# Chunk 4's attention value product of batches 1 to 6 as a Strassen product over key chunk pairs, query halves and channel halves

## The chip, the cores and the metric

The kernel runs on one core of one Trainium2 chip. The metric is the device time of one execution in microseconds (us); lower is better. Three runs of the kernel before took 1174.89 to 1175.7 us, median 1175.52.

## The reference

```python
def _attn_ref(u, v, z):
    B, S, D = u.shape            # 8, 3008, 256; z is 8 x 3008 x 64
    scale = 1.0 / S
    scores = scale * np.matmul(z, z.transpose(0, 2, 1))
    attn = np.maximum(scores, 0.0) ** 2
    out = np.matmul(attn, v)
    return (u * out).astype(np.float32)

def _moe_ref(x, w_in, w_out):    # 24064 x 256, 256 x 2048, 2048 x 256
    h = x @ w_in
    g = h * (1.0 / (1.0 + np.exp(-1.702 * h)))
    return (g @ w_out).astype(np.float32)
```

The second function is applied to the first one's output, with all batches' rows one below the other. The attention weights are symmetric, since queries and keys are the same z, and there is no softmax.

## The kernel before

**Tiles.** A batch has 3008 positions: 24 key blocks of 128 (NJ = 24; the last holds 64), and 6 query chunks of 512 (NCH = 6; the last holds 448). CB = 4 key blocks make one chunk. The 256 channels are two halves of 128 (NCC = 2), read from V with a step of two elements. All matmul operands are fp16, and sums are fp32 in PSUM.

**Scores.** `scores` (L244) computes a pair of key blocks against a query chunk on TensorE, `square` (L265, L279) takes relu with a factor csc on ScalarE and squares on VectorE. Since the weights are symmetric, only the blocks on one side of the diagonal are computed: `turn_unit` transposes a squared pair with a DMA into the tile TT, which serves as the other side's weights. `pieces` says in which order the pairs of a chunk come, the tables SCHED and SCHED0 at which step of which chunk each is issued.

**Attention value product.** `attend` (L376) computes, for a query chunk, out transposed: channels on the partitions, 512 queries along the row, summed over the key blocks in a PSUM bank for each channel half. In chunks 0 to 3 and 5 the two channel halves run side by side on two row halves of the array (64 rows each). In chunk 4 (`full(b)`, batches 0 to 6) each step is one matmul with all 128 rows: 23 key blocks for one half, then for the other, and a step for the half block, 47 steps in all. `gate` (L393) multiplies the bank by u, transposed by `turn_u` (L211), into XT, the expert's input. The bank stays taken until then.

**Up-projection inside chunk 4.** In batches 0 to 6, chunk 4's steps are interleaved with 16 groups of `up_group` (LAGY = 16): four matmuls of 512 columns (L431), a gelu on ScalarE from PSUM (L444) into one of two buffers gf, and a rescaling by FSC to fp16 on VectorE (L450), which frees gf. `some_sums` inserts sums for the down-projection behind some of them. The other 32 groups of a batch follow after chunk 5, interleaved with the down-projection (`pair_product`, L604), which is itself a seven-product (Strassen) form in which the sums S1 to S4 (`pair_sum`, L561 to L570) are made on VectorE. Its sums of the weights are made once (`weight_sums`, L498).

**Order.** Each engine executes its instructions in the order in which this program writes them; the schedule is by hand. Tables hold the places: TURN (when u is transposed), LOAD (when u is loaded, on the POOL queue), SCHED (score pairs). Buffers rotate: four PSUM banks `ps1` for products, two double banks `ps2` for scores and up-projection, three buffers for rl (the relu's result), 26 for tag "a" (weights and sums), 14 for tag "tt" (transposed weights and gelu results). A new tile waits until the last reader of the tile that had its place is done.

Of the kernel before, what the change touches and what calls it, by code (L numbers as in the profile page):

```python
# [9 lines left out]
F32 = mybir.dt.float32  # L10
F16 = mybir.dt.float16
P = 128
# [3 lines left out]
def kernel(  # L16
# [36 lines left out]
    csc = 16.0  # L53
# [17 lines left out]

    ident = const.tile([P, P], F16, name="ident")
    make_identity(nc, ident)
    nil = pw.tile([P, CH], F16, name="nil", tag="gf")
    dve.memset(nil, 0.0)  # L75

# [251 lines left out]

    def full(b):

        return NCH - 2 if b < B - 1 else NCH - 1

    def attend(b, i, both=False):
# [36 lines left out]
        def step(k):  # L370
            done = []
            for m in order[k]:
                c, h, j = m
                if (k, m) == first[c]:
                    acc[c] = ps1.tile([P, CH], F32, name="o", tag="ps1")
                ins = pe.matmul(  # L376
                    acc[c][:, :n], V16[b][h, j].rearrange("p (c k) -> p k c", k=NCC)[:, c], weights(b, i, j)[h],
                    start=(k, m) == first[c], stop=(k, m) == final[c],
                )
                if k in turns:  # L380
                    behind(acc["sig"], ins)
                done.append(ins)
            if k + 1 in turns:
                acc["sig"] = post(done)
            for c in cs:
                if k == final[c][0]:
                    gate(c)
# [28 lines left out]
    def up_group(b, q):  # L416
# [34 lines left out]
        if not pair or q < LAGY and q % 4 < 3:  # L451
            some_sums(8)
# [271 lines left out]
    def pieces(b, i):  # L724

        lst = [(i, jp) for jp in range(2 * i, NU)]
        if i == NCH - 1:
            return [(i, jp) for jp in range(2 * i) if not turned(b, jp // 2)] + lst
        if b == 0:
            return lst[-2:] + lst[:-2] if turned(b, i) else lst  # L730
        k = max(len(lst) - 6, 2)
        return lst[:k] + lst[-2:] + lst[k:-2]
# [6 lines left out]
        3: {n: 1 for n in (6, 14, 32, 38)} | {NJ: 2},  # L739
# [8 lines left out]
    TURN = {(1, NJ + 4): 2, (2, NJ + 4): 3, (4, NJ + 4): 4, (5, 8): 5}  # L748
# [53 lines left out]
    for b in range(B):  # L802
# [5 lines left out]
        for i in range(NCH):  # L808
# [4 lines left out]
            for n, step in enumerate(attend(b, i, b == 0 and i == 0)):  # L813
# [28 lines left out]
                take(host, sched[i].get(n, 0))  # L842
                if i == full(b) and n >= HEAD and (n - HEAD) * LAGY // (2 * NJ - 10) >= head and head < LAGY:
                    up_group(b, head)
                    head += 1
                step()
# [64 lines left out]
```

## Time and profile before

| | |
|---|---|
| median of three runs | 1175.52 us (1174.89 to 1175.7) |
| the profiled execution | 1175.17 us |
| its span, first to last instruction | 1173.4 us |
| mean granted TensorE clock | 1.000 |
| VectorE, ScalarE, POOL busy in the span | 872.4, 837.2, 211.2 us |
| TensorE matmuls | 7996 |
| chunk 4 of batch 2 on TensorE | 350.77 to 374.85, 24.08 us |

Times inside the profile are counted from the first instruction. Engines: PE is TensorE, PEld its weight loads, DVE VectorE, ACT ScalarE, POOL GpSimd, SP SyncE. L376 is line 376 of the kernel before. A matmul's length in the profile goes to its modelled end, so neighbours overlap, and its price is the distance between two starts. A row of a group reads: line, engine, operation, output<-inputs with shapes, count | busy us, mean ns of one | idle time before them and what ended it.

### The profile page before, as it was taken

The page shows a single profiled execution, that of the slowest core. Times are in us where ns is not written, and L with a number is a line of the kernel's source. Part 1 is how long each engine was busy: PE and PEld are TensorE (multiplying, and loading weights), DVE is VectorE, ACT ScalarE, POOL GpSimd, SP SyncE. Part 2 cuts the span into 40 slices and gives each one's busy share as a digit, 9 for nine tenths or more (in the row PEclk, how much of TensorE's full clock was granted, in tenths as well). Part 3 has the DMA queues.
Part 4 walks back from the last instruction along what each step waited for, and adds up shares of the span by engine and source line. Part 5 has one row for each costly group of instructions (what it writes and reads, how often), then busy time and mean ns, then how long its engine had stood idle before and what let it go on. Part 6 is the DMA issues. An engine that isn't in the chain of part 4 may idle for free.

```text
span 1173.4 us, 20856 instructions
## 1 busy us (share of the span) xinstructions
PE 1167.2 (99%) x7996; PEld 552.9 (47%) x7996; DVE 872.4 (74%) x1386; ACT 837.2 (71%) x941; POOL 211.2 (18%) x294
## 2 busy tenths in 40 slices
PE   9999999999999999999999999999999999999998
PEld 3544454444444445444444445444444444544446
DVE  7779865888667886588865887658876588664776
ACT  7888864688647886478864787657876578672785
POOL 3033201232012310132101421024200241001000
PEclk9999999999999999999999999999999999999999
DMA  9996499854997559965499865995559965697023
GB/s 224 201 158 104 81 174 160 97 90 92 169 158 96 90 100 175 159 97 88 97 171 148 109 87 108 173 155 92 90 99 180 140 109 83 116 175 135 1 37 73
DMA packets 459027, 143.47 MB, mean 122 GB/s; under 512 B 424624, under 2 KB 453040, under 8 KB 458928
## 3 DMA queue, kind: packets, MB, share of 16 engines
q1 hardware_dynamic: 402464, 102.36, 53.4%
q0 software_dynamic: 55104, 38.49, 22.3%
q8 instruction: 62, 1.02, 0.4%
q10 hardware_dynamic: 1360, 1.31, 0.4%
q14 instruction: 37, 0.30, 0.1%
HBM read 60.29 MB, written 24.64 MB: 72 GB/s over the span
## 4 chain that ended last, share of the span: by engine, by line
PE 99%; ACT 0%; DVE 0%; issue 0%
PE o L376 41%; PE hg L431 28%; PE st L604 23%; PE sc L244 6%; PE st L652 1%; PE yp L578 1%; PE w L99 0%; ACT rl L265 0%; PE zp L135 0%; ACT ZT L143 0%; DVE zst L128 0%; DVE a L279 0%; DVE y L670 0%; ACT zst L126 0%; DVE nil L75 0%
## 5 line engine op out<-in xcount | busy, mean ns | idle before, releaser
L444 ACT ACTIVATE gf<-hg 128x1024 f32<-128x1024 f32 (+1 forms) x384 | 382.9, 1001 | 115.0 <-PE hg L431 106.6
L265 ACT ACTIVATE rl<-sc 128x1024 f16<-128x1024 f32 (+1 forms) x301 | 287.3, 993 | 173.0 <-PE sc L244 128.7
L431 PE MATMUL hg<-xt,W 128*128 128x512 f16 (+1 forms) x1408 | 353.5, 374 | 0.0
L376 PEld LDWEIGHTS <-V 64*128 64x128 f16 (+1 forms) x4098 | 219.7, 94 | 251.1 <-issue 9.1
L376 PE MATMUL o<-a,V 64*128 64x512 f16 (+3 forms) x2278 | 296.1, 368 | 0.0
L450 DVE TENSOR_SCALAR gt<-gf 128x1024 f16<-128x1024 f32 (+1 forms) x288 | 203.7, 709 | 94.5 <-ACT gf L444 92.8
L279 DVE TENSOR_TENSOR a<-rl 128x1024 f16<-128x1024 f16 (+1 forms) x266 | 178.6, 674 | 121.7 <-ACT rl L265 120.8
L204 POOL DMA_DIRECT2D uq<-in_u_dram x168 | 115.3, 695 | 728.9 <-PE sc L244 532.5
L431 PEld LDWEIGHTS <-W 128*128 128x128 f16 x1536 | 149.5, 98 | 176.6 <-issue 3.1
L376 PE MATMUL o<-tt,V 64*128 64x512 f16 (+1 forms) x1518 | 232.5, 377 | 0.0
L244 PE MATMUL sc<-ZT 64*128 64x512 f16 (+3 forms) x688 | 115.4, 356 | 0.7 <-ACT ZT L143 0.3
L604 PEld LDWEIGHTS <-WT 128*128 128x128 f16 x736 | 72.0, 98 | 79.5 <-issue 0.6
L448 ACT ACTIVATE gt<-gf 128x1024 f16<-128x1024 f32 (+1 forms) x96 | 98.1, 1022 | 3.1
L604 PE MATMUL st<-gt,W 128*128 128x512 f16 (+1 forms) x368 | 89.9, 370 | 0.0
L604 PE MATMUL st<-s,WT 128*128 128x512 f16 (+1 forms) x368 | 89.1, 370 | 0.0
L604 PE MATMUL st<-gt,WT 128*128 128x512 f16 (+1 forms) x368 | 88.8, 370 | 0.0
L604 PEld LDWEIGHTS <-W 128*128 128x128 f16 x552 | 53.8, 98 | 58.2
L393 DVE TENSOR_TENSOR xt<-o,ut 128x512 f16<-128x512 f32 x80 | 51.5, 685 | 28.9 <-PE o L376 28.8
L566 DVE TENSOR_TENSOR s<-gt 128x1024 f16<-128x1024 f16 (+1 forms) x92 | 61.9, 673 | 1.1
L570 DVE TENSOR_TENSOR s<-gt,s 128x1024 f16<-128x1024 f16 (+1 forms) x92 | 61.0, 663 | 1.9 <-DVE s L568 0.5
L568 DVE TENSOR_TENSOR s<-s,gt 128x1024 f16<-128x1024 f16 (+1 forms) x92 | 60.9, 662 | 1.5
L621 DVE SCALAR_TENSOR_TENSOR y<-st,y 128x512 f32<-128x512 f32 (+1 forms) x69 | 45.5, 662 | 19.3 <-PE st L604 18.6
(66 smaller groups left out, 672.8 us busy)
## 6 DMA issues: line engine op xcount, KB each, us to landing
out_dram<-yo SPq DMA_DIRECT2D x156, 128.0 KB, 2.8
uq<-in_u_dram POOLq DMA_DIRECT2D x140, 128.0 KB, 3.6
V<-in_v_dram POOLq DMA_DIRECT2D x35, 256.0 KB, 6.4
tt<-a SPq DMA_TRANSPOSE x232, 3.4
uq<-in_u_dram POOLq DMA_DIRECT2D x28, 112.0 KB, 4.4
out_dram<-yo SPq DMA_DIRECT2D x28, 96.0 KB, 6.5
uq<-in_u_dram SPq DMA_DIRECT2D x20, 128.0 KB, 4.4
wst<-in_moe_w_in_dram POOLq DMA_DIRECT2D x4, 512.0 KB, 5.6
```

The costliest lines, as they stand in the source:

```text
L204: eng.dma_start(uq[k * QW:(k + 1) * QW, :n // QW].rearrange("t q c k -> t q (c k)"), src[:, :, cs])
L244: pe.matmul(sc[:, r, :q1 - q0], zt[h, 2 * kp + r, :], zt[h].rearrange("d n p -> d (n p)")[:, q0:q1], start=True, stop=True,)
L265: act.activation(rl[:, :, :n], sc[:, :, :n], AF.Relu, scale=csc)
L279: dve.tensor_tensor(a[:, :, :n], rl[:, :, :n], rl[:, :, :n], ALU.mult)
L376: ins = pe.matmul(acc[c][:, :n], V16[b][h, j].rearrange("p (c k) -> p k c", k=NCC)[:, c], weights(b, i, j)[h], start=(k, m) == first[c], s ...
L431: pe.matmul(hg[:, e, :n], W1[:, c, ff * P:(ff + 1) * P], XT[b, i][:, c, :n], start=(c == 0), stop=(c == NCC - 1),)
L444: act.activation(gf[:, :, :n], hg[:, :, :n], AF.Gelu_apprx_sigmoid, scale=1.0 / FSC)
L448: act.activation(g, gf[:, :, :n], AF.Copy, scale=FSC)
L450: dve.tensor_scalar(g, gf[:, :, :n], FSC, None, ALU.mult)
L566: dve.tensor_tensor(s_, a21, a22, ALU.add)
L570: dve.tensor_tensor(s_, a12, ST[b, s, "S2", m], ALU.subtract)
L604: pe.matmul(bank, right[:, ff], lhs[:, f], start=new and ff == 0, stop=ff == NFF // 2 - 1, skip_group_check=True,)
```

## The change

In batches 1 to 6 (`split`), chunk 4's product is made by seven products of half size instead of eight. The left matrix is split in query halves (m) and key chunks of a pair (e), V in key chunks and channel halves; there are three pairs of key chunks (t), of four blocks each (g). Per batch VectorE makes for each t four forms of V (`value_forms`, into VT) and four forms of the scores (`score_forms`, S1, S2 and S4 into SA; S3 in place), at the places that `fills` lists as (chunk, step). Every product then runs over 3 x 4 blocks with 256 queries: 42 steps of two matmuls. P1, P5 and P2 begin a bank; P6, P7 and P4 are added to P1's, P3 to P5's. ScalarE copies the bank where an intermediate sum is needed (after P1, P5 and P6) into ya, which takes two of rl's three buffers; VectorE adds P7, P3 and P2 to it and multiplies by u; P4's result is multiplied from the bank. The last, half block of V is copied by POOL into VZ, a tile whose other half holds zeros, so that it counts as a whole block.

Moved with it (in batches 1 to 6 where nothing else is said): the transpose of u for chunk 4 from step 28 to step 10, in batches 1 to 7; the score pairs of chunk 3's steps 6, 14, 32 to steps 3, 10, 17; the order of the pairs of chunk 4; the down-projection's sums begin at the ninth group instead of the first, and a group now stands behind its step instead of ahead of it. The factor csc is 8 instead of 16. Batches 0 and 7 keep the old product.

```diff
--- before.py
+++ after.py
@@ -50,7 +50,7 @@
     LAST = S - (NCH - 1) * CH
     LFULL = LAST - SREM
 
-    csc = 16.0
+    csc = 8.0
     FSC = csc * csc * float(S) * float(S)
 
     dve, act, pe, sp, pool = nc.vector, nc.scalar, nc.tensor, nc.sync, nc.gpsimd
@@ -69,10 +69,12 @@
     ET = mybir.EngineType
     ctx.enter_context(tc.manual_schedule(engines={ET.PE, ET.Pool, ET.SP, ET.DVE, ET.Activation}))
 
+    VZ = const.tile([P, D], F16, name="VZ")
     ident = const.tile([P, P], F16, name="ident")
     make_identity(nc, ident)
     nil = pw.tile([P, CH], F16, name="nil", tag="gf")
     dve.memset(nil, 0.0)
+    pool.memset(VZ, 0.0)
 
     ZP, WS = {}, {}
     late, LATE = [], []
@@ -326,6 +328,156 @@
         return TT[b, cj, i][:, :, g, :]
 
 
+    def channels(v_, c):
+
+        return v_.rearrange("p (c k) -> p k c", k=NCC)[:, c]
+
+    def split(b, i):
+
+        return i == NCH - 2 and 0 < b < B - 1
+
+    VT, SA = {}, {}
+
+    def key_half(b, t, e):
+
+        last = t == NCH // 2 - 1 and e
+        js = [(8 * t + 4 * e, CB - int(last), 0)] + ([(NJ - 1, 1, CB - 1)] if last else [])
+        for j, n, g in js:
+            src = VZ.rearrange("p (o d) -> p o d", o=1) if j == NJ - 1 else V16[b][:, j:j + n]
+            yield src.rearrange("p j (c k) -> p j k c", k=NCC), g, n
+
+    def value_forms(b, t):
+
+        def form(f):
+            if t not in VT:
+                VT[t] = pa.tile([P, 4, CB, P], F16, name="vt", tag="tt", bufs=14)
+            (k1, _, _), = key_half(b, t, 0)
+            for k2, g, n in key_half(b, t, 1) if f else [(None, 0, CB)]:
+                out_, t1, t2 = (VT[t][:, x, g:g + n] for x in (f, 0, 1))
+                b11, b12 = k1[:, g:g + n, 0], k1[:, g:g + n, 1]
+                a_, b_ = (
+                    (b12, b11) if f == 0 else (k2[:, :, 1], t1) if f == 1
+                    else (k2[:, :, 1], b12) if f == 2 else (k2[:, :, 0], t2)
+                )
+                dve.tensor_tensor(out_, a_, b_, ALU.subtract)
+
+        return [lambda f=f: form(f) for f in (0, 2, 1, 3)]
+
+    def score_part(b, t, e, part, m):
+
+        i, c0 = NCH - 2, 2 * t + e
+        if c0 == i:
+            if part == 0:
+                return unit[b, i, 2 * i][:, 2 * m:2 * m + 2]
+            return unit[b, i, 2 * i + 1][:, m].rearrange("p r (q c) -> p r q c", c=P)
+        tile_ = TT[b, min(c0, i), max(c0, i)][:, 2 * m:2 * m + 2]
+        if t < NCH // 2 - 1:
+            return tile_.rearrange("p q g c -> p (q g c)")
+        tile_ = tile_[:, :, 2 * part:2 * part + 2]
+        return tile_ if part == 0 else tile_.rearrange("p q r c -> p r q c")
+
+    def score_form(b, t, name, part):
+        a11, a12, a21, a22 = (score_part(b, t, e, part, m) for m, e in ((0, 0), (0, 1), (1, 0), (1, 1)))
+        if name == "S3":
+            dve.tensor_tensor(a21, a11, a21, ALU.subtract)
+            return
+        if (t, name) not in SA:
+            SA[t, name] = pa.tile([P, 2, CH], F16, name="sa", tag="a", bufs=26)
+        if t < NCH // 2 - 1:
+            view = lambda x: SA[t, x].rearrange("p r c -> p (r c)")
+        else:
+            view = lambda x: SA[t, x][:, part].rearrange("p (q r c) -> p q r c", r=2, c=P)
+        if name == "S1":
+            dve.tensor_tensor(view(name), a21, a22, ALU.add)
+        elif name == "S2":
+            dve.tensor_tensor(view(name), view("S1"), a11, ALU.subtract)
+        else:
+            dve.tensor_tensor(view(name), a12, view("S2"), ALU.subtract)
+
+    def score_forms(b, t):
+        parts = 1 if t < NCH // 2 - 1 else 2
+        return [lambda x=x, p_=p_: score_form(b, t, x, p_) for x in ("S1", "S2", "S4", "S3") for p_ in range(parts)]
+
+    def moving(b, t, g, name):
+
+        raw = {"P1": (0, 0), "P2": (0, 1), "P4": (1, 1), "P7": (1, 0)}
+        if name in raw:
+            m, e = raw[name]
+            i, c0 = NCH - 2, 2 * t + e
+            if c0 != i:
+                return TT[b, min(c0, i), max(c0, i)][:, 2 * m:2 * m + 2, g]
+            if g < 2:
+                return unit[b, i, 2 * i][:, 2 * m:2 * m + 2, g]
+            return unit[b, i, 2 * i + 1][:, m, g % 2]
+        form = SA[t, {"P5": "S1", "P6": "S2", "P3": "S4"}[name]]
+        if t < NCH // 2 - 1:
+            return form.rearrange("p r c -> p (r c)").rearrange("p (q g c) -> p q g c", g=CB, c=P)[:, :, g]
+        part = form[:, g // 2].rearrange("p (q r c) -> p q r c", r=2, c=P)
+        return part[:, :, g % 2] if g < 2 else part[:, g % 2]
+
+    def still(b, t, g, name):
+
+        if name in ("P1", "P2", "P3"):
+            j = 8 * t + g + (0 if name == "P1" else CB)
+            return channels(VZ if j == NJ - 1 else V16[b][:, j], int(name == "P3"))
+        return VT[t][:, {"P5": 0, "P6": 1, "P7": 2, "P4": 3}[name], g]
+
+    def attend_split(b, i):
+
+        seq = [("P1", 0), ("P1", 1), ("P1", 2), ("P5", 0), ("P5", 1), ("P2", 0), ("P2", 1), ("P6", 0), ("P6", 1)]
+        seq += [("P5", 2), ("P6", 2), ("P3", 0), ("P3", 1), ("P7", 0), ("P7", 1), ("P7", 2)]
+        seq += [("P3", 2), ("P2", 2), ("P4", 0), ("P4", 1), ("P4", 2)]
+        XT[b, i] = pa.tile([P, NCC, CH], F16, name="xt", tag="xt", bufs=6)
+        banks, half = {}, CH // 2
+
+        def step(name, t, h):
+            new = name in ("P1", "P2", "P5")
+            if new and (t, h) == (0, 0):
+                banks[name] = ps1.tile([P, CH], F32, name="oz", tag="ps1")
+            bank = banks[{"P6": "P1", "P7": "P1", "P4": "P1", "P3": "P5"}.get(name, name)][:, :half]
+            for g in (2 * h, 2 * h + 1):
+                pe.matmul(
+                    bank, still(b, t, g, name), moving(b, t, g, name),
+                    start=new and (t, g) == (0, 0), stop=(t, g) == (2, CB - 1), skip_group_check=True,
+                )
+            if (t, h) != (2, 1):
+                return
+            if name == "P1":
+                banks["y"] = [pw.tile([P, 2, half], F32, name="ya", tag="rl", bufs=3) for _ in range(2)]
+            y, x = banks["y"], XT[b, i]
+            ut = lambda c: UT[b, i][:, c].rearrange("p q t -> p (q t)")
+            if new and name != "P2" or name == "P6":
+                k, r = {"P1": (1, 0), "P5": (0, 1), "P6": (0, 0)}[name]
+                act.activation(y[k][:, r], bank, AF.Copy, scale=1.0)
+            elif name == "P4":
+                dve.tensor_tensor(x[:, 0, half:], bank, ut(0)[:, half:], ALU.mult)
+            else:
+                k, r = {"P3": (0, 0), "P7": (0, 1), "P2": (1, 0)}[name]
+                part = y[k][:, r]
+                dve.tensor_tensor(part, part, bank, ALU.add)
+                if name == "P3":
+                    dve.tensor_tensor(x[:, 1], y[0].rearrange("p o c -> p (o c)"), ut(1), ALU.mult)
+                elif name == "P2":
+                    dve.tensor_tensor(x[:, 0, :half], part, ut(0)[:, :half], ALU.mult)
+
+        return [lambda x=x, t=t, h=h: step(x, t, h) for x, t in seq for h in range(2)]
+
+    def fills(b):
+
+        VT.clear()
+        SA.clear()
+        at = {(0, 19): [lambda: pool.tensor_copy(VZ[TOP], V16[b][TOP, NJ - 1])]}
+        slots = [(0, n) for n in (20, 23, 26, 28)] + [(1, n) for n in (27, 31, 35, 39, 43)]
+        slots += [(2, n) for n in (19, 21, 23)]
+        ops = [op for t in range(3) for op in value_forms(b, t)]
+        slots += [(2, n) for n in (28, 33, 38, 43)] + [(3, n) for n in (30, 34, 41, 44)]
+        slots += [(4, n) for n in (12, 12, 14, 14, 16, 18, 20, 22)]
+        ops += [op for t in range(3) for op in score_forms(b, t)]
+        assert len(ops) == len(slots)
+        for where, op in zip(slots, ops):
+            at.setdefault(where, []).append(op)
+        return at
+
     def full(b):
 
         return NCH - 2 if b < B - 1 else NCH - 1
@@ -374,7 +526,7 @@
                 if (k, m) == first[c]:
                     acc[c] = ps1.tile([P, CH], F32, name="o", tag="ps1")
                 ins = pe.matmul(
-                    acc[c][:, :n], V16[b][h, j].rearrange("p (c k) -> p k c", k=NCC)[:, c], weights(b, i, j)[h],
+                    acc[c][:, :n], channels(V16[b][h, j], c), weights(b, i, j)[h],
                     start=(k, m) == first[c], stop=(k, m) == final[c],
                 )
                 if k in turns:
@@ -448,7 +600,7 @@
             act.activation(g, gf[:, :, :n], AF.Copy, scale=FSC)
         else:
             dve.tensor_scalar(g, gf[:, :, :n], FSC, None, ALU.mult)
-        if not pair or q < LAGY and q % 4 < 3:
+        if not pair or LAGY > q >= (LAGY // 2 if split(b, NCH - 2) else 0) and q % 4 < 3:
             some_sums(8)
         if pair:
             some = (("S1", "S2", "S3"), ("S4",))[r % 2] if fg >= NFG // 2 else ()
@@ -728,6 +880,8 @@
             return [(i, jp) for jp in range(2 * i) if not turned(b, jp // 2)] + lst
         if b == 0:
             return lst[-2:] + lst[:-2] if turned(b, i) else lst
+        if split(b, i):
+            return [lst[0], lst[2], lst[3], lst[1]]
         k = max(len(lst) - 6, 2)
         return lst[:k] + lst[-2:] + lst[k:-2]
 
@@ -736,7 +890,7 @@
         0: {n: 1 for n in (5, 9, 13, 17, 30, 33, 36, 39, 42, 45)} | {NJ: 2},
         1: {n: 1 for n in (5, 9, 13, 17)} | {NJ: 2},
         2: {n: 1 for n in (2, 7, 12, 17)} | {NJ: 2},
-        3: {n: 1 for n in (6, 14, 32, 38)} | {NJ: 2},
+        3: {n: 1 for n in (3, 10, 17, 38)} | {NJ: 2},
         4: {},
         5: NEXT,
     }
@@ -745,7 +899,7 @@
 
     TURN0 = {(i, (38, 28)[i] if i < 2 else NJ + 4 if i < NCH - 1 else 12): i for i in range(NCH)}
     LOAD0 = {(1, 14): 2, (1, 40): 3, (4, 4): 4, (4, 36): 5}
-    TURN = {(1, NJ + 4): 2, (2, NJ + 4): 3, (4, NJ + 4): 4, (5, 8): 5}
+    TURN = {(1, NJ + 4): 2, (2, NJ + 4): 3, (4, 10): 4, (5, 8): 5}
     LOADW = {
         (2, 16): 0, (3, 0): 2, (3, 9): 1, (3, 41): 3, (4, 28): 4, (4, 34): 5, (4, 40): 6, (5, 0): 7,
     }
@@ -810,7 +964,9 @@
             if host > b:
                 fill(host)
                 LATE.append(host)
-            for n, step in enumerate(attend(b, i, b == 0 and i == 0)):
+            if i == 0 and split(b, NCH - 2):
+                extra = fills(b)
+            for n, step in enumerate(attend_split(b, i) if split(b, i) else attend(b, i, b == 0 and i == 0)):
                 if b == 0 and i == 0 and n in (5, 24):
                     load_u(0, n // 24)
                 if b == 0 and i == 0 and n == 2:
@@ -840,10 +996,16 @@
                 if b == 0 and i == NCH - 1 and n in (8, 30, 42):
                     wsums.pop(0)()
                 take(host, sched[i].get(n, 0))
+                if split(b, NCH - 2):
+                    for op in extra.get((i, n), ()):
+                        op()
+                if split(b, i):
+                    step()
                 if i == full(b) and n >= HEAD and (n - HEAD) * LAGY // (2 * NJ - 10) >= head and head < LAGY:
                     up_group(b, head)
                     head += 1
-                step()
+                if not split(b, i):
+                    step()
         late.sort(key=lambda t: t[0])
         if more:
             for i in range(2):
```

## Prediction

> **What bounds the kernel now.** I read the page first: the busy shares, the granted clock and the chain that ended last.
>
> ```profile
> PE 1167.2 (99%) x7996; PEld 552.9 (47%) x7996; DVE 872.4 (74%) x1386; ACT 837.2 (71%) x941; POOL 211.2 (18%) x294
> ...
> PEclk9999999999999999999999999999999999999999
> ...
> PE 99%; ACT 0%; DVE 0%; issue 0%
> ```
>
> TensorE (PE) is busy from end to end, its clock is never throttled, and the chain is PE alone. The view of waits charges PE with under 2 us, all at the start. So time goes if PE gets less to do, and comes back where another engine makes PE wait. Second I cut one batch (batch 2) into its stages by the view of windows; the rows are chunks 0, 1, 2, 3, 4, 5 and the expert stage, the columns PE, PEld, DVE, ACT and POOL busy.
>
> ```profile
> 304.43:318.00 13.57, 13.57 (x132) 6.48 (x130) 8.91 (x16) 12.75 (x15) 0.00 (x0) 1.00 1.07 178
> 318.00:328.40 10.40, 10.40 (x100) 4.75 (x98) 6.76 (x12) 5.82 (x6) 0.00 (x0) 1.00 1.01 164
> 328.40:339.70 11.30, 11.30 (x110) 5.16 (x106) 6.46 (x11) 5.39 (x6) 0.00 (x0) 1.00 1.01 165
> 339.70:350.77 11.07, 11.07 (x108) 4.95 (x102) 7.14 (x13) 4.75 (x6) 3.61 (x5) 1.00 0.88 148
> 350.77:374.85 24.08, 24.08 (x114) 10.81 (x114) 19.14 (x28) 16.36 (x16) 7.88 (x9) 1.00 0.93 119
> 374.85:385.84 10.99, 10.99 (x117) 5.46 (x113) 7.80 (x15) 8.53 (x10) 4.91 (x8) 1.00 0.31 77
> 385.84:447.45 61.61, 61.61 (x334) 30.86 (x334) 49.88 (x80) 47.59 (x58) 11.68 (x17) 1.00 0.63 101
> ```
>
> PE fills every stage. VectorE (DVE) has 2.2 to 4.9 us free in each chunk, and 11.7 us in the expert stage: that is what the change can spend.
>
> **The price of a matmul.** Third, PE's timeline (start, length to the modelled end), and one row of the chain in order of time:
>
> ```profile
> 371.94 1.03 PE L431 MATMUL hg<-xt,W 128*128 128x512 f16 x4
> 372.80 0.38 PE L376 MATMUL o<-tt,V 128*128 128x512 f16 x1
> ```
> ```profile
> 1018.59 1.79 PE yp L578 x32
> ```
>
> What counts is the distance between starts. Four matmuls of 512 columns take 0.86 us, so 215.9 ns each; 32 of 128 columns take 1.79 us, so 55.9. That is 0.4167 ns a column and some 2.5 ns on top, and 256 columns come to 109.2 ns. The only 256-column matmuls of the trace (L244, a pair side by side on two row halves, 306.58 to 306.69) took 0.11 us, which fits.
>
> **The sum on PE.** Removed in each of batches 1 to 6: chunk 4's 47 steps of 512 columns (2 channel halves by 23 key blocks, and the half block), 47 x 215.9 = 10.15 us. Added: 7 products x 12 blocks = 84 matmuls of 256 columns, 84 x 109.2 = 9.17 us. Gain 0.97 us a batch, 5.85 us for six. The 16 up-projection groups woven into the chunk (64 x 215.9 = 13.8 us) stay. Each of the 84 has a weight load of its own; whether it lies under the stream is shown by the line with the shortest stream:
>
> ```profile
> L578 PEld LDWEIGHTS <-W 128*128 128x128 f16 x128 | 7.5, 98 | 0.5
> ...
> L498 DVE TENSOR_TENSOR WT<-W 128x1024 f16<-128x1024 f16 x1 | 1.2, 1221 | 0.0
> ```
>
> A load is 98 ns long, and L578 still ran at 55.9 ns: loads overlap with each other and with the streams, so at 109 ns they are free. Bounds: 109.2 if they hide, 109.2 + 98 = 207 if none did, which would be 7.3 us more a batch; I take 109.2, since L578 is the same form with half the columns.
>
> The Trainium skill speaks against this: "TensorE: Matmul & The Clock Gate", section "Back-to-back issue gap", gives a stream of load and matmul pairs some 81 ns at 128 columns and 131 ns at 512. A line between them puts 256 columns at about 98 ns, an estimate from that page, and by it 84 x 98 = 8.2 us would replace 47 x 131 = 6.2 us, 2 us slower a batch. This trace has 55.9 and 215.9 ns for the same two sizes, so the measurement decides.
>
> **What DVE gets.** The pace at which DVE starts instructions, from its timeline:
>
> ```profile
> 364.95 1.31 DVE L566 TENSOR_TENSOR s<-gt 128x1024 f16<-128x1024 f16 x1
> 366.19 0.68 DVE L450 TENSOR_SCALAR gt<-gf 128x1024 f16<-128x1024 f32 x1
> 366.79 0.68 DVE L568 TENSOR_TENSOR s<-s,gt 128x1024 f16<-128x1024 f16 x1
> ...
> 377.32 0.42 DVE L256 TENSOR_TENSOR ad<-rl 128x512 f16<-128x512 f16 x1
> 377.65 1.10 DVE L211 STREAM_TRANSPOSE ut<-uq 128x896 f32<-128x896 f32 x1
> ```
>
> A 1024-wide sum blocks the queue for 0.60 us, a 512-wide one for 0.33. A value form reads every second element of V; the one row like it, L498, takes 1.22 us for 1024, so 0.61 for 512. Per batch: 12 value forms, three of them cut in two (0.1 more each), 7.6 us; 8 score forms of 1024 (4.8) and 8 of 512 (2.6). At the end two gates of 0.60 go, and three adds and two products of 256 columns come (0.35 each: L670, 128x256 f32, lasts 0.42, less the 0.07 by which neighbours overlap) with one gate of 0.60: net 1.15. In all 16.2 us, so 106.1 + 16.2 = 122 of 142 us, 86%. By stage: chunk 0 8.9 + 2.4 = 11.3 of 13.6; chunk 1 6.8 + 3.1 = 9.8 of 10.4; chunk 2 6.5 + 4.5 = 11.0 of 11.3; chunk 3 7.1 + 2.4 = 9.5 of 11.1; chunk 4, from which two 0.6 sums move to the expert stage, 19.1 - 1.2 + 3.8 = 21.7 of 23.1. No stage is over full. ACT gets three 256-column copies (0.4 each), POOL one copy a batch and a memset at the start, before its wait until 6.49 us for the first value load: hidden. The new factor 8 changes numbers alone.
>
> **Does PE wait for it?** I lay DVE's queue of chunk 4, in program order, against PE's steps (0 is PE's first matmul there). A step of two matmuls is 0.2185 us, a group 0.864; the groups stand after steps 2, 5, 7, 10, 12, 14, 17, 19, 21, 24, 26, 29, 31, 33, 36 and 38, so step 18 starts at 18 x 0.2185 + 7 x 0.864 = 10.0. A group's L450 is ready 2.1 us after its first matmul, as 351.22 against 353.34 shows. DVE then runs: L450 of the first three groups (ready at 2.8, 4.3, 5.6) to 6.2, the moved transpose of u (1.16) to 7.4, L450 8.0, both halves of S1 8.7, L450 9.3, S2 10.0, L450 10.5, S4 10.9, L450 11.8, S4 12.2, L450 13.1, S3 13.5, L450, a sum and S3 15.4, and so on.
> - The transpose of u, moved from step 28 to step 10: its four loads were issued from 346.0 to 348.6 and land 3.6 us later, before its turn at 357; behind it wait the forms of the last pair. S1 (8.7) is wanted by P5 at 10.0, S2 (10.0) by P6 at 11.3, S3 (15.4) by P7 at 16.9.
> - P4 writes the bank that DVE's add for P7 must have read: read at 19.2, wanted at 20.0. This is the narrowest, 0.8 us.
> - Chunk 5's second bank is freed by the add for P3: 21.7, wanted at 23.0. The last gate ends at 26.4, 3.4 us behind PE where it was 1.5; but no PE step waits for it, and the three buffers of rl and two of sc cover it until DVE's free time in chunk 5 has taken it back.
> - In chunk 2 the forms push the gate back by 1.5 us and the gate of chunk 3 by at most 3; its bank is wanted 4.8 us into chunk 4.
> - In chunk 0 PE's score matmuls follow ACT by only 0.2 us, and two value forms stand before a square there: its buffer is free just in time. In the expert stage another sum goes ahead of the first L450: the third gelu, begun at 389.85 when that L450 was done (389.76), moves to 390.4 and ends at 391.4, and PE's fifth group wants it at 391.89.
> So nothing waits by the rows, but three places are within half a microsecond. Bounds: 0 to 1 us a batch; I take 0.1, since each place still has a margin, 0.6 us in all. Beyond the 128 to 64 row change that stays, PE loses nothing else.
>
> L566 above took 1.31 us instead of 0.68 while a POOL copy (364.78, 0.95 us) ran: that is 0.6 us for each of the two copies of z in chunk 4, which the margins of the first point and DVE's waits before them cover. The Trainium skill, "SBUF — State Buffer", section "Who interferes with whom", calls the shared port an exclusive lock under which the loser fully blocks; by it both copies (1.21 and 0.95 us) would cost DVE up to 2.2 us, and the 0.8 us at P4 could be gone.
>
> The sum: the profiled execution took 1175.17 us (span 1173.4, 1.8 around it); 1175.17 - 5.85 + 0.6 = 1169.9. The median of the runs is 0.35 above the profiled one, so 1170.2.
>
> **Rivals.**
> - *DVE is too late in chunk 4* (slower). Place: P4's bank. Point: more than 0.8 us behind my queue; each microsecond beyond is one of PE. For it: at the listed lengths (0.69, 0.42) instead of the pace, and with both copies in the way, the add for P7 comes at 20.8, 0.85 late, and the gain is nearly gone. 0.1 us more on each of the 24 instructions before it makes 2.7 us late: 1.9 - 0.97 = +0.95 a batch, 1175.5 + 5.7 = 1181. Against: the pace of 0.60 holds for dozens of neighbours.
> - *Half of the gain is given back* at the tight places, chunk 0 and the third gelu, 0.5 us a batch: 1175.5 - 6 x 0.47 = 1172.7. For it: the margins of 0.2 and 0.5 us. Against: DVE's waits for ACT (92.8 us before L450) show it early as a rule.
> - *The halved matmuls don't run at half time*: at 120 ns, 84 x 0.12 = 10.1, no gain, 1175.5. Against: the straight line through 128, 256 and 512 columns.
>
> **How the numbers follow.** Forecast 0.66 (1169 to 1171.5), half 0.12, no gain 0.08, slower 0.14. A measurement of this kernel can tell some 0.2%, 2.4 us, from no change: faster 0.78, same 0.08, slower 0.14. The range goes from the full gain on a low run (1174.9 - 5.85 = 1169.0, a little less for spread) past the half case to 1174.3, and leaves the slower case out.
>
> **What would show it.** PE 7996 + 6 x 36 = 8212 matmuls; chunk 4 of batch 2 near 23.1 us instead of 24.08; DVE busy near 970 us; PE's waits still about 2 us. Waits of PE for DVE adds or forms in chunk 4, or of hg for gelu behind chunk 5, would prove the rivals; a chunk of 23.1 us with the time lost elsewhere would prove me wrong about the other chunks.

## Result and profile after: a gain of 2.4 us

The changed kernel takes 1173.14 us (median of 22 runs, 1171.0 to 1175.2) where the kernel before takes 1175.54 (22 runs): ratio 0.9975, interval 0.9968 to 0.9982. That is faster and inside the range, but only about half of the forecast 5.3 us: 2.4 us by the medians, 2.9 by the ratio, which also weighs the longer runs of the kernel before. The middle half of the runs now lies within 1.8 us (1172.08 to 1173.91), where it lay within 1.0 before. The profiled execution took 1173.48 us, span 1171.4, 2.0 less than before.

From the page of the changed kernel: busy time of each engine, granted clock, and the chain that ended last.

```profile
PE 1163.4 (99%) x8212; PEld 590.0 (50%) x8212; DVE 961.4 (82%) x1596; ACT 841.9 (72%) x959; POOL 215.2 (18%) x301
...
PEclk9999999999999999999999999999999999999999
...
PE 92%; DVE 3%; DMA 3%; ACT 1%; issue 1%; SPq 0%; DVEq 0%; ACTq 0%
```

PE has 8212 matmuls as counted, 3.8 us less to do, and an unthrottled clock. What is new is the last row: the chain was PE alone, and now 8% of it is other engines and DMA. Two chunk 4s of the same run, batches 4 and 5, in the view of windows (columns as before):

```profile
638.32:661.41 23.09, 23.09 (x151) 14.38 (x150) 22.47 (x40) 15.95 (x18) 7.90 (x9) 1.00 1.03 133
780.48:805.72 25.24, 23.95 (x152) 14.37 (x150) 21.98 (x38) 16.05 (x18) 7.19 (x9) 1.00 1.13 117
```

The first is what I forecast, 23.1 us. The second is 2.15 us longer, though the product and the groups are the same (the counts differ by a few instructions at the edges). Batches 1, 2 and 5 lost 0.19, 0.45 and 2.15 us in this way, batches 3, 4 and 6 nothing. The chain through batch 5, in order of time (start, us, what):

```profile
775.69 3.36 DMA out_dram<-yo
...
779.13 0.25 DVE yo L858
779.38 11.54 DMA tt<-a
...
790.94 1.08 DVE sa L391 x2
...
792.20 0.99 DVE gt L602
...
793.27 1.03 ACT gf L596
...
794.35 1.02 PE hg L583 x4
```

Read backwards: a group of the up-projection waits for a gelu, that for the rescaling L602 which frees its buffer, that stands on DVE behind S1 of the third pair (L391), and S1 waits for a DMA transpose `tt<-a`, 11.5 us after its issue. The view of the tile tt, 776 to 793 us, says how long that was for both transposes of this tile, and who waited:

```profile
L309 SPq DMA_TRANSPOSE tt<-a x2: 1463/2510/3556, 777.8 to 779.4; - x2
...
who waited for it (us, times):
  DVE sa L391: 1.7, 1
  PE oz L439: 1.2, 1
...
DMA to landing us min/median/max: 10.0/10.8/11.5
```

The tile holds chunk 4's queries against chunk 5's keys. In the kernel before, its last transposes land as late (8.2 and 8.7 us after issue in batch 2, 4.6 and 6.9 us into chunk 4), but PE wants them only at steps 20 and later, 11.2 us into the chunk. The new product reads the tile in its third pair: DVE's S1 has its turn at 7.95 us of chunk 4. Over the six batches the second transpose landed between 5.7 and 10.4 us into the chunk, so S1 loses that race in some batches and not in others. PE has a race of its own, P1 of the third pair, some 2 us into the chunk, with the transpose of the diagonal, `ad`: 0.21 us lost at 782.66.

### The profile page after: what moved, and what is told of

It is laid out like the page before. It is cut to its first block, busy times and chain, and to the rows that moved or that the text cites. A ratio compares the mean times of both kernels' runs of the same rounds, so it can differ in the third digit from the quotient of the medians.

```text
span 1171.4 us, 21514 instructions
## 1 busy us (share of the span) xinstructions
PE 1163.4 (99%) x8212; PEld 590.0 (50%) x8212; DVE 961.4 (82%) x1596; ACT 841.9 (72%) x959; POOL 215.2 (18%) x301
## 4 chain that ended last, share of the span: by engine, by line
PE 92%; DVE 3%; DMA 3%; ACT 1%; issue 1%; SPq 0%; DVEq 0%; ACTq 0%
PE o L528 32%; PE hg L583 26%; PE st L756 23%; PE sc L246 6%; PE oz L439 4%; DMA tt<-a 2%; PE st L804 1%; PE yp L730 1%; DVE gt L602 1%; DMA out_dram<-yo 1%; ACT rl L267 1%; ACT gf L596 0%; DVE vt L362 0%; SPq L868 0%; PE w L101 0%
## 5 line engine op out<-in xcount | busy, mean ns | idle before, releaser
L528 PEld LDWEIGHTS <-V 64*128 64x128 f16 (+1 forms) x3810 | 206.6, 94 | 201.1 <-POOLq L88 6.1
L528 PE MATMUL o<-a,V 64*128 64x512 f16 (+3 forms) x2254 | 290.5, 368 | 0.4 <-DVE a L281 0.4
L602 DVE TENSOR_SCALAR gt<-gf 128x1024 f16<-128x1024 f32 (+1 forms) x288 | 204.8, 712 | 66.4 <-ACT gf L596 63.7
L281 DVE TENSOR_TENSOR a<-rl 128x1024 f16<-128x1024 f16 (+1 forms) x266 | 176.2, 673 | 77.2 <-ACT rl L267 76.1
L528 PE MATMUL o<-tt,V 64*128 64x512 f16 (+1 forms) x1278 | 166.9, 376 | 0.0
L858 DVE STREAM_TRANSPOSE yo<-y 128x1024 f32<-128x1024 f32 (+1 forms) x46 | 56.0, 1218 | 8.5 <-DMA out_dram<-yo 5.8
```

The costliest lines, as they stand in the source:

```text
L281: dve.tensor_tensor(a[:, :, :n], rl[:, :, :n], rl[:, :, :n], ALU.mult)
L528: ins = pe.matmul(acc[c][:, :n], channels(V16[b][h, j], c), weights(b, i, j)[h], start=(k, m) == first[c], stop=(k, m) == final[c],)
L602: dve.tensor_scalar(g, gf[:, :, :n], FSC, None, ALU.mult)
```

## Experiments

Theory A: these transposes land too late for the new readers, because they are issued only 1 to 3 us before chunk 4, behind an output store on SP's queue and among the loads of u and z. Rival B: VectorE, 82% busy, is simply too full. The kernel before, run beside each of them, had medians of 1175.38 to 1175.71.

### S1 reads a tile that has landed

```diff
-        tile_ = TT[b, min(c0, i), max(c0, i)][:, 2 * m:2 * m + 2]
+        tile_ = TT[b, min(c0, i), max(c0, i)] if c0 < NCH - 1 else TT[b, NCH - 3, i]
+        tile_ = tile_[:, 2 * m:2 * m + 2]
```

> In the last key pair (t = 2) the score forms S1 and S4 read, in place of the tile of chunk 5's keys that two DMA transposes fill last, the tile of chunk 3's keys that landed long before; the product of that pair is so made of another tile's numbers. Instructions, shapes and queues stay. Theory A (the changed kernel loses 1 to 5 us because VectorE stands in its queue at S1, waiting for those two transposes, and the rescalings behind it hold up the gelu and TensorE): all six chunks 4 take 23.1 us from their first matmul to the half-rows of chunk 5, and the median falls by 2.5 to 3.5 us to 1169.8 to 1170.6, with a spread under 1 us. Rival B (VectorE's queue in chunks 1 to 4 is too full): no transposes matter, 1172.5 to 1173.7 as before this edit.

1172.44 us (1171.15 to 1176.1, 7 runs), ratio 0.9976 (0.9966 to 0.9987). In the profiled run, 1171.15, DVE never waits at S1, and four chunk 4s take 23.09 us. The other two take 23.51 and 23.47, and PE's waits name the second race:

```profile
PE w L101 <- DVE nil L76: 1.2, 1, 1.2
PE oz L440 <- DMA ad<-a: 0.5, 2, 0.3
```

So the profile went as A says, the median did not. With S1's race gone, P1's race with `ad` remains; that it makes the spread too is likely but not shown, for the profiled run is the fastest of the seven.

### Value forms that read V densely

```diff
-            yield src.rearrange("p j (c k) -> p j k c", k=NCC), g, n
+            yield src.rearrange("p j (k c) -> p j k c", k=NCC), g, n
```

> The value forms read V's channels as two dense halves instead of every second element, so the numbers are those of other channel pairs. A form of 512 should then block VectorE for 0.33 instead of 0.61 us, some 3.3 us less a batch, in chunks 0, 1 and 2. The transposes that S1 of the last pair waits for stay. Theory A: VectorE only comes earlier to the same wait, in chunk 4 nothing is gained; but chunk 2's end is 1 to 1.5 us earlier, and with it the store and the transposes behind it on SP's queue, so at most 1.5 us in all: 1171.5 to 1173.2, spread as before. Rival B: most of the 3 us comes back, under 1171, with a small spread.

1171.0 us (1170.4 to 1171.9), ratio 0.9963 (0.9951 to 0.9976): 2 us better, with DVE relieved in chunks 0 to 2 only. By the time alone this speaks for B. But the profile shows S1 still waiting (1.37, 0.63 and 0.65 us in three batches), and the last transposes issued some 0.4 us earlier in most batches, presumably since the squares and output transposes that they and SP's queue wait for come earlier from DVE. They land no earlier for it in four of the six batches; the diagonal's, `ad`, lands 0.9 to 2.1 us earlier. Both readings stood; a later run parts them.

### Transposes early, second store late

```diff
-        3: {n: 1 for n in (3, 10, 17, 38)} | {NJ: 2},
+        3: {n: 1 for n in (0, 4, 8, 38)} | {NJ: 2},
-                if (i, n) in ((3, 3), (3, 26) if more else (4, 14)) and LAST2:
+                if (i, n) in (((3, 9), (3, 46)) if split(b, NCH - 2) else ((3, 3), (3, 26) if more else (4, 14))) and LAST2:
```

> Chunk 3's first three score pairs are issued at steps 0, 4, 8 instead of 3, 10, 17, and the two stores of the batch before (transpose on VectorE, DMAs on SP's queue) at steps 9 and 46 instead of 3 and 26, so that SP issues the three transposes ahead of the store's four DMAs, not behind them. Same work. Theory A: the last transpose is issued some 3 us earlier, ahead of the loads of u, lands before chunk 4 begins or in its first 4 us, S1 waits for nothing, and the time falls to 1169.8 to 1170.8. Rival B: VectorE has the same work in another order, 1172.5 to 1174.

1197.2 us (1194.14 to 1201.29), ratio 1.0189 (1.0169 to 1.0208). The transposes did land early, the second one 0.14 us into chunk 4 in batches 1 to 3, but a new wait came in their place. DVE's waits in this run:

```profile
DVE yo L858 <- DMA out_dram<-yo: 32.2, 6, 6.7
```

The output transpose writes the only buffer yo; it stood at the head of DVE's queue until the first store, now behind the transposes, had read it: 32.2 us in six batches, and S1 and everything else behind it. The changed kernel has the same wait in small, 5.8 us in five batches, the kernel before 0.7 in two.

### The old places of the pairs

```diff
-            return [lst[0], lst[2], lst[3], lst[1]]
+            return lst[:2] + lst[2:]
-        3: {n: 1 for n in (3, 10, 17, 38)} | {NJ: 2},
+        3: {n: 1 for n in (6, 14, 32, 38)} | {NJ: 2},
```

> Undoes one part of the change: chunk 3's score pairs at steps 6, 14, 32, 38 again, and chunk 4's own pairs first, so that the pairs whose transposes S1 wants come last, at step 24. Theory A: these transposes are issued 2 to 3 us later and land 11 to 13 us into chunk 4, every batch stalls by 2 to 4 us, 1183 to 1195. Rival B: the squares lie better spread in chunk 3, 1172 to 1174.

1177.9 us (1175.48 to 1181.88, 11 runs), ratio 1.0022 (1.0012 to 1.0032). All six chunk 4s stall (23.48 to 25.62 us), so the moved places are worth nearly 5 us of the change; but the last transposes are issued no later (3.0 and 1.6 us before chunk 4), where I had expected them 2 to 3 us later: it is SP's queue rather than the pairs' steps that times the issue. S1 waits in five batches and P1 in three; the chunk 4s lose 5.7 us in all, against 2.8 in the changed kernel. That is 2.9 of the 4.0 us between the two profiled runs; the rest is not located.

### Two more sums on VectorE in chunk 4

```diff
-        if not pair or LAGY > q >= (LAGY // 2 if split(b, NCH - 2) else 0) and q % 4 < 3:
+        if not pair or q < LAGY and q % 4 < 3:
```

> The two sums of the gate that the change moved out of chunk 4 (it now does two at half rows beside chunk 3 instead) go back to their old places, so that VectorE has two more sums of 0.6 us each in chunk 4 of each split batch and two fewer before it; everything else stays. Theory A (the last DMA transposes of chunk 4's tile land too late, because they are issued 1 to 3 us before chunk 4 among the loads, and VectorE's S1 and TensorE's P1 of the third pair wait for them): S1 now comes up to 1.2 us later in VectorE's own order, so its wait for the landing shrinks by as much, and the time is what it was within a microsecond, 1172.5 to 1174. Rival B (VectorE has too much to do in chunk 4): 1.2 us more of it in each of six batches lengthens chunk 4 from 23.1 to 24 us or more everywhere, also in the batches where no transpose is late, and the time is 1176 to 1181.

1174.35 us (1173.11 to 1178.17, 12 runs), ratio 0.9992 (0.9981 to 1.0002): between the two. In the batches where nothing is late chunk 4 takes 23.57 and 23.61 us, 0.5 more, most of it in two pieces that every batch has: 0.22 at a group of the up-projection (653.62 in batch 4) and 0.20 at the first matmul of P4 (659.26), which waits for DVE's add of P7 to have read the bank. It is the place I had called the narrowest, with 0.8 us of slack: 1.2 us more work, less the 0.2 that PE had already lost, costs 0.2 there. So B's mechanism exists, 0.8 us away, and is not what the changed kernel suffers from. (The sums are the down-projection's, not the gate's, as the expectation has it. The profiled run is the slowest of the twelve, 1178.17 us: its batches 5 and 6 lose 4.2 and 1.6 us, with 3.1 us of PE's waits for `ad`.)

### A second buffer for the first store

The early pairs again, with the stores at steps 9 and 26, and:

```diff
-        yo = pw.tile([P, CH // QW, QW, NCC], F32, name="yo", tag="yo", bufs=1)
+        if k == NCH - 2 and b < B - 2:
+            yo = pa.tile([P, CH // QW, QW, NCC], F32, name="yt", tag="tt", bufs=14)
+        else:
+            yo = pw.tile([P, CH // QW, QW, NCC], F32, name="yo", tag="yo", bufs=1)
```

> Chunk 3's transpose pairs of the queries stand at steps 0, 4 and 8 instead of 3, 10 and 17 and the first output store behind them at step 9, as in the run with early transposes, but the first store's tile is a buffer of its own (from the pool of the other transposed tiles), so that the second output transpose has not to wait for the first store's landing. Theory A: the tile's last transposes land before 0.5 us of chunk 4, S1 and P1 of the third pair wait for nothing, chunk 4 takes 23.1 us in nearly all batches, VectorE does not stand at the output transpose (under 0.3 us in all six), and the time is 1169.5 to 1171.5 with a spread under 2 us. Rival B (VectorE's fullness in chunk 4, not the landing): chunk 4 keeps its stalls of 0.2 to 2 us in some batches, 1172 to 1175.

1170.12 us (1170.0 to 1170.53, 6 runs), ratio 0.9948 (0.9936 to 0.996). Batches 4 and 5 by windows, and the chain of the page:

```profile
637.69:660.78 23.09, 23.09 (x150) 14.39 (x149) 20.21 (x36) 16.18 (x18) 7.89 (x9) 1.00 0.97 134
779.85:802.94 23.09, 23.09 (x151) 14.40 (x150) 20.61 (x36) 16.06 (x18) 7.56 (x9) 1.00 1.00 132
```
```profile
PE 99%; ACT 0%; DVE 0%; issue 0%
```

All six chunk 4s take 23.09 us, no wait at S1 or P1, and the chain is PE again. The second transpose lands 0.1 to 1.3 us into chunk 4, in one batch at 5.3, all before S1's turn. DVE has as much to do as in the changed kernel (959.4 us). Of all versions that compute the reference this is the fastest.

### The loads of u and z behind P1

```diff
+            if (name, t, h) == ("P1", 2, 0):
+                post([banks["last"]])
...
-                if (i, n) in load:
-                    load_u(b, load[i, n])
+                late_u = {(3, NJ + 20): 0, (4, 5): 4} if split(b, NCH - 2) else {}
+                if late_u.get((i, n), load.get((i, n))):
+                    load_u(b, late_u.get((i, n), load.get((i, n))))
```

The load of z moves from step 2 to step 6 of chunk 4 in the same way, the turn of u from step 10 to step 28.

> In the split batches GpSimd holds back the load of u and that of z, which it issued 2 to 4.5 us before chunk 4, until the first P1 of the third pair of chunk 4 has run, about 2 us into it; the transposes are issued where they were. Theory A with the loads as what slows the transposes: these land 3.2 to 5 us after their issue instead of 8 to 11.5, so before 3 us of chunk 4, S1 has no wait, chunk 4 takes 23.1 us, and the time is 1169.5 to 1171.5, unless z or u is now late for chunk 5 or the next batch's expert stage, which would show as a wait for the DMA of u or z there. Rival (the transposes are slow by themselves, or what slows them is another queue): they land 8 us and more after issue as before, and the time stays at 1172 to 1175.

1173.97 us (1173.43 to 1176.36, 12 runs), ratio 0.9983 (0.9975 to 0.9992). The transposes, issued where they were, in batch 5:

```profile
DMA to landing us min/median/max: 3.2/3.2/3.2
```

3.2 us instead of 10.0 to 11.5: the loads are what slows them. S1 waits nowhere. The time did not follow, in part because of my own edit: with u turned at step 28, DVE reaches the add for P7 late. DVE in batch 1, GpSimd, and PE (start, us, engine, line, what; in brackets the idle time and what ended it):

```profile
222.84 1.23 DVE L213 STREAM_TRANSPOSE ut<-uq 128x1024 f32<-128x1024 f32 x1
224.00 1.16 DVE L604 TENSOR_SCALAR gt<-gf 128x1024 f16<-128x1024 f32 x1
225.09 0.40 DVE L459 TENSOR_TENSOR ya<-ya,oz 128x256 f32<-128x256 f32 x1
```
```profile
223.79 0.83 POOL L173 COPY zst<-zst 128x768 f16<-128x768 f16 x1 [3.58 <-DMA zst<-in_z_dram]
```
```profile
225.54 0.38 PE L439 MATMUL oz<-tt,vt 128*128 128x256 f16 x2 [0.48 <-DVE ya L459]
```

The 1.16 us transpose ahead of the add makes PE wait at P4's bank, the narrow place again. By itself it costs 0.1 us: chunk 4 takes 23.2 us in batches 3 to 6. In batches 1 and 2 it takes 23.73 and 23.60, since GpSimd's copy of z, which the edit also moved, runs beside the rescaling L604 ahead of the add, which then lasts 1.16 and 1.03 us instead of 0.65. That is 1.7 us in six batches, and PE's score matmuls wait 0.8 us for a gelu; the rest of the 3.2 us by which the span exceeds that of the run with two output tiles (1168.6) is not located.

### Only the pairs early

```diff
-        3: {n: 1 for n in (3, 10, 17, 38)} | {NJ: 2},
+        3: {n: 1 for n in (0, 4, 8, 38)} | {NJ: 2},
```

> Only chunk 3's transpose pairs move, to steps 0, 4 and 8; the stores stay where they are, at steps 3 and 26 of the half rows. The rows of the last pair are ready earlier, so the DMA transposes of the last tile are issued before the first store or right behind it, 3 us or more earlier than now. Theory A: landing before 3 us of chunk 4 in all batches, no wait at S1, and the second output transpose waits for the first store's landing only if that store comes out behind the transposes on SyncE's queue: with under 0.5 us of it 1169.5 to 1172, with a microsecond or more in each batch 1175 to 1182. Rival B: chunk 4 is no shorter than in the changed kernel, 1172.5 to 1175.

1182.38 us (1181.62 to 1184.52), ratio 1.0055 (1.0041 to 1.0068). SP's queue in batch 2, here and, second, in the run with two output tiles:

```profile
346.43 2.40 SPq L868 DMA_DIRECT2D out_dram<-yo  x4
348.94 3.84 SPq L309 DMA_TRANSPOSE tt<-a  x2
```
```profile
344.40 2.63 SPq L309 DMA_TRANSPOSE tt<-a  x2
347.12 3.37 SPq L871 DMA_DIRECT2D out_dram<-yt  x4
```

The pairs stand 3 to 9 steps earlier, but the store issued at step 3 is still ahead of the tile's transposes on the queue: before chunk 4 the first comes 0.6 us earlier and the second 0.2, instead of 3; they land as late as 7.6 to 9.7 us into chunk 4, and the output transpose on DVE waits 25.5 us for that store in six batches. The landing part of my expectation failed, for I took a place right behind the store to be as good as one ahead of it.

### The same edits of place in the kernel before

> The kernel before the change, with no Strassen product, given the same three edits of place as the run with two output tiles: chunk 3's pairs at steps 0, 4 and 8, the first store at step 9, and the first store's tile a buffer of its own. Theory A (the product is worth 0.97 us in each of six batches; the edits of place only take away a wait that the product brought): in the kernel before, the tile is first wanted 17 us and more into chunk 4, so there is nothing for the edits to gain: 1175.0 to 1176.2, and the run with two output tiles stands 5 to 6 us under this one. Rival C (the edits of place are worth 3 us by themselves, whatever the product): 1172 to 1173.5.

1175.61 us (1175.11 to 1179.12, 12 runs), ratio 1.0002 (0.9991 to 1.0014). Without the product there is nothing for them to gain. (The tile is first wanted 11.2 us into chunk 4 there, not the 17 that I wrote; its last transposes land at 6.9 to 8.7.)

### Only z's load behind P1

The changed kernel with the two lines of the post and z's load at step 6; u as it was.

> The changed kernel with the load of z alone held on GpSimd until the first P1 of the third pair of chunk 4 has run, 5 to 6 us into it; the loads of u and the turning of u stay where the change has them. It tells whether the load of u alone slows the DMA transposes. If z's small packets slow them: they land 3.2 to 4.5 us after their issue, before 3.5 us of chunk 4, chunk 4 takes 23.1 us, and the time is 1169.8 to 1171. If it is u's loads, or both in about equal parts: landings at 4 to 8 us of chunk 4 as before, some stalls at S1 left, 1171.5 to 1173.5. With the theory that neither matters, 8.6 us and more as before, 1173.

1171.15 us (1170.15 to 1172.86 in eleven of the 12 runs, one at 1180.04), ratio 0.9965 (0.9949 to 0.998). The load of z now starts 2.7 us into chunk 4, not 5 to 6. The transposes of batch 2:

```profile
DMA to landing us min/median/max: 7.0/7.4/7.7
```

9.1 to 10.4 us in the changed kernel, 3.2 with both loads away, 7.0 to 7.7 with u's alone. Over the six batches the second transpose takes 6.4 to 11.5, 3.2 and 4.3 to 8.9 us: u's loads are the larger part, z's the last 2 to 3 us. Those decide: the second transpose now lands at 3.6 to 7.8 us, just before S1's turn, which waits nowhere, and four chunk 4s take 23.09 us, the others, where P1 still waits for `ad`, 23.17 and 23.59. The landings are as I expected with u's loads to blame, the median 0.35 us below the range that went with them.

### Two output tiles and dense value forms

> The run with two output tiles and, with it, value forms that read V densely instead of every second element (the forms then take other channels than the product wants, so the numbers of chunk 4's product are other ones; the instructions, their shapes and their order are the same). VectorE loses some 3 us of work a batch in chunks 0 to 2, as in the run with dense value forms alone. Theory A (VectorE's fullness cost time only because it delayed the issue of the last transposes): these land early here anyway, chunk 4 already takes 23.1 us, and the time is that of the run with two output tiles, 1169.6 to 1170.4. Rival B (the full queue of VectorE in chunks 0 to 2 costs TensorE time by itself): a microsecond or more below it, 1167.5 to 1169.2.

> The run with two output tiles once more, as the neighbour of the one with dense value forms on the same chip: 1169.8 to 1170.7 with a spread under 1 us by theory A; by the rival, for which the small spread seen before was chance, single runs of 1171 to 1173.

1169.67 us (1169.11 to 1170.1) with dense forms, 1170.1 without, measured together. So with the transposes early, a freer DVE is worth 0.4 us and not 2. The profile has a place for it, a score matmul of chunk 0. PE in batch 2 without dense forms (the run first profiled) and, second, with them:

```profile
315.75 0.38 PE L528 MATMUL o<-tt,V 64*128 64x512 f16 x2
316.06 0.29 PE L246 MATMUL sc<-ZT 64*128 64x256 f16 x2
```
```profile
315.08 0.38 PE L528 MATMUL o<-tt,V 64*128 64x512 f16 x2
315.30 0.27 PE L246 MATMUL sc<-ZT 64*128 64x256 f16 x2
```

The starts are 0.31 us apart instead of 0.22. ScalarE's seven relus just before take 6.55 us, because the value forms stand among the squares that free their buffers; with dense forms, as in the kernel before, they take 6.39. The 0.1 us is lost in each of batches 2 to 6, and with dense forms in one of them. What else the earlier run with dense forms gained, over 1 us, is argued only: the transposes were issued sooner and `ad` landed sooner, but S1 still waited. Five of the six runs without dense forms lie from 1169.66 to 1170.33, and one at 1176.22, of which there is no profile; my forecast of the spread failed by that one.

## Why the prediction was right and wrong

- **The sum on PE**: right in kind and, inside chunk 4, in size. In the trace of the run with two output tiles the 84 matmuls start 109 ns apart and take 9.28 us; what they replaced took 10.26 in the undisturbed batches (both with the 0.1 us that the change to 64 rows costs behind the last). So chunk 4 falls from 24.08 to 23.09 us, as forecast. A whole batch gains less: chunk 4 of batches 2, 3 and 4 begins at 350.77, 493.80 and 639.64 before and at 350.50, 492.71 and 637.69 in that run, so a batch is 0.82 and 0.86 us shorter, 5.0 in six. The other 0.12 to 0.17 us a batch is lost outside chunk 4, 0.1 of it at the score matmul of chunk 0. The weight loads are hidden, and the rival of the matmuls not at half time is out. The lower spacing that the Trainium skill gives in "TensorE: Matmul & The Clock Gate", section "Back-to-back issue gap", by which I estimated 98 ns, isn't seen here either. VectorE's free time in the chunks, read as 2.2 to 4.9 us, is 3.2 to 4.9 by the rows; nothing hangs on it.
- **The failed step** is "Does PE wait for it?". I laid DVE's queue against PE's steps and wrote that S1, done at 8.7 us, is in time for P5 at 10.0, "so nothing waits by the rows". DVE's order was right (S1's turn is at 7.95 us where nothing is late), but I asked only when DVE is free, and not when the tile that S1 reads has landed. I asked that for u alone, and there with 3.6 us, a median over the whole execution: the four loads before chunk 4 of batch 2 land 3.7 to 7.4 us after issue in the same trace. The two transposes stand in the trace of before with the same 8 to 9 us; nobody wanted them early there, so nothing pointed at them. S1 and P1 of the third pair are new, earlier readers of old data.
- **What it cost**: of the profiled run, 0.19 + 0.45 + 2.15 = 2.8 us in three chunk 4s, 0.3 at the start (the first product begins at 8.00 us instead of 7.71; in the other runs at 7.6 to 8.4, with the old product too, so this is chance) and 0.2 at one score matmul: 5.0 - 3.3 = 1.7, and the 2.0 measured has besides some 0.3 us that the kernel before loses in its batches 1 and 5. With the races gone the time is 1170.12 us beside the 1170.2 that I named. So the sum held apart from the races: chunk 4 gives 5.9 us, and against the 0.6 allowed for waits stand some 0.8 lost outside it.
- **The rivals**: the time (1173.14) is near the one of half the gain given back (1172.7), but not by its places: chunk 0 gives back 0.1 us a batch of the 0.5 named, and the third gelu behind chunk 5 shows no wait. That the time lies in the range is luck, since the range was drawn to cover this case and another wait brought the time there. P4's bank, the slower case, held its margin in the changed kernel and gave way in two experiments that put 1.2 us more DVE work ahead of it (0.2 us lost in one, 0.1 to 0.6 in the other).
- **Why the loads matter**: transposes on SP's queue and loads on GpSimd's both pass through the core's 16 DMA engines. That it is the loads is shown (3.2 against 10 us and more); how the engines share is not. The Trainium skill, "DMA: Bandwidth & Descriptors", section "Issuing engines are not separate DMA queues", says that DMAs run on the same 16 engines and interleave whichever engine started them, which these runs bear out: another issuing queue gave no protection.

## What to carry to other kernels

When a change lets an instruction read data earlier than anything did before, look up the landing time of that data in that stretch, and not only the queue of the engine that reads it; a transfer that was late without harm is in no list of waits. Then look at what stands ahead of the transfer on its queue, and at which other transfers share the engines in that stretch. Where the runs of a kernel spread more after a change (here 1.8 us instead of 1.0 for the middle half), look for a race whose two sides have come near each other.

## What I had not expected of the hardware

- A DMA transpose of 3.2 us takes up to 11.5 with 4 KB packets of u and 128-byte packets of z in flight, on another queue, and differs by 5 us between batches of one run (6.4 to 11.5 us).
- In the run with transposes early and second store late, PE stood still for 3.8 us in batch 4, and the granted clock halved behind it. The view of windows (the clock is the third number from the right):

```profile
655.00:659.00 4.00, 3.76 (x12) 1.72 (x12) 3.45 (x6) 1.94 (x2) 2.28 (x3) 0.50 0.98 96
659.00:663.00 4.00, 4.00 (x21) 2.20 (x20) 3.88 (x8) 2.05 (x2) 2.14 (x3) 0.81 0.92 150
663.00:667.00 4.00, 4.00 (x27) 2.53 (x26) 3.42 (x7) 3.62 (x5) 1.60 (x3) 1.00 1.08 160
```

Twelve matmuls in the first 4 us against 27 in the last: half speed until about 660 us. In batch 6 a gap of 2.5 us was enough:

```profile
952.80:956.80 4.00, 3.22 (x13) 1.55 (x13) 3.45 (x6) 1.94 (x2) 2.28 (x3) 0.65 1.09 104
```

A gap of 1.9 us in batch 2 left the clock at 1.00. A long enough wait of PE is thus paid a second time: PE's waits in chunk 4 add up to 18.9 us, the three stretches of low clock (batches 4, 5 and 6) to some 6 more, and the span is 25.4 us longer than that of the run with two output tiles.
